# The second FFN's units set one unit further behind the first FFN's

## The chip, the cores and the metric

The kernel runs on one core of one Trainium2 chip. The metric is the device time of one execution in microseconds (us), lower is better; the median of several runs is given, and beside it one execution that the hardware profiler recorded.

## What is computed

For two batches of 3008 tokens of width 256, a squared-ReLU attention, then two feed-forward networks (FFNs) on all 6016 tokens:

```python
scores = (1.0 / S) * np.matmul(z, z.transpose(0, 2, 1))      # z: 64 wide
attn   = np.maximum(scores, 0.0) ** 2
x      = u * np.matmul(attn, v)                              # B*S = 6016 rows of 256
h      = x @ w_in                                            # 256 -> 2048
y      = (h - np.tanh(h)) @ w_out                            # 2048 -> 256
gate   = 1.0 / (1.0 + np.exp(-(y @ w_gate)))                 # 256 -> 1536
out    = (gate * (y @ w_val)) @ w2_out                       # 1536 -> 256
```

The FFN weights come as 64-bit floats and are decoded on the core. Each matmul of the FFNs is done as three matmuls of rounded high and low parts (names ending in h and l: yh, yl; gh, gl).

## The kernel before

The 6016 tokens are cut into 12 chunks (`chunks`): five of 512 tokens and one of 448 in each batch, so chunks 5 and 11 are short. All work on PE is cut into **units**, and the program is written unit by unit, in an order that a table of numbers sets.

- `Attention` and `HalfAttention`: two key tiles of a chunk, 12 units a chunk.
- `Ffn1(c, f)` (L391): 256 of the first FFN's 2048 inner columns of chunk c, 8 units a chunk. Its `front` (L399) is 12 matmuls into a PSUM tile `h`; `mid1` (L405) turns h into th (four instructions of ACT: th, sq, sq, m; three of DVE: e, th, th); `mid2` (L419) splits th into gh (ACT) and gl (DVE); `back` (L428) is 12 matmuls of gh and gl with w_out into two accumulators `acc` in PSUM. After the last unit of a chunk, `end` (L434) splits the accumulators into yh and yl, the input of the second FFN.
- `Ffn2(c, f)` (L443): 128 of the 1536 inner columns of chunk c, 12 units a chunk. `front` (L451) is 12 matmuls into `gv`; `mid1` one sigmoid on ACT (sg, L461) and one product on DVE (L462); `mid2` the split into p (ACT L467, DVE L81); `back` (L471) is 6 matmuls of p into its own pair of accumulators. After a chunk's last unit `end` (L474) copies the two accumulators to `o` with two ACT instructions (L479) and stores o with two DMAs of SP's queue (L480).

`accumulate` (L227, matmul at L235) and `project` (L243, matmul at L247) issue the FFNs' matmuls. The accumulators of both FFNs come from the pool `psa` (L72), which has two pairs of banks; a new pair is taken at the `back` of a chunk's first unit (L620 to L622). `front`'s tiles come from `psf`, also two.

The main loop takes one unit a step. In step n it writes, in this order: the helpers due at n (loads, splits of weights and of x), `front` and `mid1` of unit n, `mid2` of unit n-1, the `end` of a chunk whose last `back` was in the step before (`LATE` is 1), and `back` of unit n-3. Each engine runs its instructions in the order in which they are written.

The order of the units around the last attention chunk and in the FFNs is `mixed` (L486 to L490): every unit gets a number and the units are sorted by it, the first FFN ahead of the second at equal numbers. Unit f of chunk c of the second FFN has the number 19.5 + 12c + f + LAG; unit f of chunk c of the first FFN 19.5 + 12(c - 1) + 1.5f (for c of 1 and more). With LAG = 7 the last unit of a chunk of the second FFN (f = 11) and the first unit of its next chunk stand next to each other.

Loads of x (`load_x`, 8 units ahead of the first FFN's chunk) and its split (`split_x`, 3 units ahead) hang on the first FFN's units; the splits of the second FFN's weights (L561 to L564) on the second FFN's units of chunk 0, 3 units ahead. Weights, x, y and o live in 41 slots of the pool `ring`.

Of the kernel before, what the change touches and what calls it, by code (L numbers as in the profile page):

```python
# [30 lines left out]
def squared_relu_attention__then__two_ffns(  # L31
# [31 lines left out]
    SPLIT = 9  # L63
    START = 11.5
    LAST = 7.5
    LAG = 7

    ring = ctx.enter_context(tc.tile_pool(name="ring", bufs=41))
    work = ctx.enter_context(tc.tile_pool(name="work", bufs=10))
# [418 lines left out]
    mixed += [(KP + LAST + (c - 1) * N2 + f * N2 / N1, 1, Ffn1(c, f)) for c in range(1, NC) for f in range(N1)]  # L488
    mixed += [(KP + LAST + c * N2 + f + LAG, 2, Ffn2(c, f)) for c in range(NC) for f in range(N2)]
    units += [t[2] for t in sorted(mixed, key=lambda t: t[:2])]  # L490
# [178 lines left out]
```

## Time and profile before

| | |
|---|---|
| median of 3 runs | 1656.49 us (1656.0 to 1656.74) |
| the profiled execution | 1654.31 us, span 1652.5 us |
| PE busy | 1593.4 us, 96% of the span |
| DVE, ACT busy | 67%, 63% of the span |
| granted clock of PE, mean | 0.982 |
| DMA | 32 GB/s mean |

The span runs from the first to the last instruction. PE is the matrix engine, PEld its weight loads, DVE the vector, ACT the scalar engine; SP issues the DMAs. In a chain of waits, the work that ended last is followed back from the last instruction, at each step to what released it; a timeline lists the instructions in order of time and in brackets the idle time before them with what ended it. Granted clock 1.00 is 2.4 GHz, 0.50 is 1.2 GHz.

### The profile page before, as it was taken

How to read it: one execution, taken by the hardware profiler on the slowest of the kernel's cores; microseconds unless marked ns; L12 is line 12 of the kernel's file. 1: busy time of each engine (PE TensorE's matmuls, PEld its weight loads, DVE VectorE, ACT ScalarE, POOL GpSimd, SP SyncE). 2: the span in 40 equal slices, each digit the busy share in tenths (PEclk: the TensorE clock that was granted, in tenths of full speed). 3: DMA queues.
4: the chain of work that ended last, by engine and by line, in shares of the span. 5: the costliest groups of instructions: out<-in, count | busy, mean ns of one | idle time of the engine just before them, and what ended most of it. 6: DMA issues, size and time to landing. Idle time of an engine off the chain costs nothing.

```text
span 1652.5 us, 21852 instructions
## 1 busy us (share of the span) xinstructions
PE 1593.4 (96%) x9120; PEld 1371.7 (83%) x9120; DVE 1106.0 (67%) x1255; ACT 1038.4 (63%) x1251; POOL 0.2 (0%) x4
## 2 busy tenths in 40 slices
PE   9999999999999998998989989898998989989898
PEld 7888899999998887887878878787887878878788
DVE  8988889888789775564555555465555655656433
ACT  8767778776789776565555556566555656556422
POOL 0000000000000000000000000000000000000000
PEclk9999999999999999999999999999999999999999
DMA  6222232221010000000000000000000000000000
GB/s 217 78 78 77 83 109 76 77 78 52 25 39 25 0 1 13 26 1 24 1 13 13 1 26 0 24 3 12 13 1 26 0 13 12 0 13 0 13 1 24
DMA packets 28179, 53.31 MB, mean 32 GB/s; under 512 B 1968, under 2 KB 10160, under 8 KB 28080
## 3 DMA queue, kind: packets, MB, share of 16 engines
q1 hardware_dynamic: 28080, 51.91, 9.2%
q8 instruction: 71, 1.16, 0.3%
q14 instruction: 28, 0.23, 0.0%
HBM read 39.58 MB, written 12.32 MB: 31 GB/s over the span
## 4 chain that ended last, share of the span: by engine, by line
PE 93%; DVE 3%; ACT 3%; issue 1%; DVEq 0%; ACTq 0%
PE acc L235 27%; PE gv L247 24%; PE acc L364 22%; PE h L247 14%; PE s L321 6%; DVE th L416 1%; DVE th L417 1%; ACT sq L413 1%; DVE e L81 1%; DVE gl L81 1%; ACT sq L412 1%; ACT th L411 1%; ACT p L467 0%; ACT o L479 0%; PE acc L584 0%
## 5 line engine op out<-in xcount | busy, mean ns | idle before, releaser
L364 PE MATMUL acc<-ah,v 64*128 64x512 f32 (+1 forms) x2212 | 322.7, 383 | 0.0
L81 DVE TENSOR_TENSOR e<-h,th 128x1024 f32<-128x1024 f32 (+1 forms) x96 | 115.3, 1201 | 281.7 <-ACT sq L412 281.7
L235 PE MATMUL acc<-p,wo 128*128 128x512 f32 (+1 forms) x864 | 229.9, 404 | 52.5 <-ACT o L479 52.5
L364 PEld LDWEIGHTS acc<-ah,v 64*128 64x128 f32 x2212 | 246.7, 184 | 19.2
L235 PEld LDWEIGHTS acc<-p,wo 128*128 128x128 f32 x864 | 168.8, 197 | 89.1 <-ACT o L479 58.4
L461 ACT ACTIVATE sg<-gv 128x512 f32<-128x512 f32 (+1 forms) x144 | 84.6, 588 | 240.3 <-PE gv L247 240.1
L247 PE MATMUL h<-xh,wi 128*128 128x512 f32 (+1 forms) x768 | 233.7, 385 | 0.0
L411 ACT ACTIVATE th<-h 128x1024 f32<-128x1024 f32 (+1 forms) x96 | 96.8, 1008 | 210.9 <-PE h L247 210.9
L462 DVE TENSOR_TENSOR sg<-gv,sg 128x512 f32<-128x512 f32 (+1 forms) x144 | 97.7, 679 | 179.8 <-ACT sg L461 179.8
L235 PE MATMUL acc<-gh,wo 128*128 128x512 f32 (+1 forms) x768 | 204.2, 385 | 0.0
L364 PE MATMUL acc<-al,v 64*128 64x512 f32 (+1 forms) x1106 | 200.3, 383 | 0.0
L333 ACT ACTIVATE a<-s 128x1024 f32<-128x1024 f32 (+2 forms) x142 | 142.3, 1003 | 86.1 <-PE s L321 54.9
L81 DVE TENSOR_TENSOR al<-a,ah 128x1024 fp32r<-128x1024 f32 (+3 forms) x146 | 173.5, 1188 | 11.3 <-DVE ah L338 0.5
L247 PE MATMUL gv<-yh,wg 128*128 128x512 f32 (+1 forms) x576 | 180.1, 395 | 0.0
L247 PE MATMUL gv<-yh,wv 128*128 128x512 f32 (+1 forms) x576 | 175.7, 386 | 0.0
L247 PEld LDWEIGHTS h<-xh,wi 128*128 128x128 f32 x768 | 144.1, 188 | 27.5 <-ACT a L281 0.3
L235 PEld LDWEIGHTS acc<-gh,wo 128*128 128x128 f32 x768 | 144.2, 188 | 27.1
L336 ACT ACTIVATE a<-a 128x1024 f32<-128x1024 f32 (+2 forms) x142 | 147.7, 1041 | 4.4
L247 PE MATMUL h<-xl,wi 128*128 128x512 f32 (+1 forms) x384 | 147.9, 385 | 0.0
L364 PEld LDWEIGHTS acc<-al,v 64*128 64x128 f32 x1106 | 131.8, 184 | 9.8 <-DVE al L81 0.2
L417 DVE COPY_PREDICATED th<-m,e 128x1024 f32<-128x1024 uint32 (+1 forms) x96 | 131.2, 1366 | 9.9
L247 PEld LDWEIGHTS gv<-yh,wg 128*128 128x128 f32 x576 | 112.3, 195 | 21.8
(98 smaller groups left out, 2211.7 us busy)
## 6 DMA issues: line engine op xcount, KB each, us to landing
raw_wo<-w_out SPq DMA_DIRECT2D x14, 512.0 KB, 5.7
u<-uT SPq DMA_DIRECT2D x10, 512.0 KB, 6.7
x<-u SPq DMA_DIRECT2D x10, 512.0 KB, 3.0
xl<-x SPq DMA_DIRECT2D x10, 512.0 KB, 3.3
outT<-o SPq DMA_DIRECT2D x20, 256.0 KB, 2.1
vraw<-v SPq DMA_DIRECT2D x9, 512.0 KB, 6.9
raw_wi<-w_in SPq DMA_DIRECT2D x8, 512.0 KB, 8.2
zraw<-zT SPq DMA_DIRECT2D x12, 256.0 KB, 6.4
```

Source lines behind the costliest of these rows:

```text
L81: nc.vector.tensor_tensor(out=out, in0=a, in1=b, op=ALU.subtract)
L235: nc.tensor.matmul(acc[d][:, :n], wt[:, wi, w, d * P : (d + 1) * P], hl[ai], start=first and m == 0, stop=last and m == len(passes) - 1,)
L247: nc.tensor.matmul(ps, w[:, wi, d, fi * P : (fi + 1) * P], xs[xi][:, d, :n], start=m == 0, stop=m == len(passes) - 1)
L321: nc.tensor.matmul(self.ps[:, e, :n], z_t[b, i // 4][r, ki ^ x, c : c + P], q[r, qi ^ x, :n], start=m == 0, stop=m == 2)
L333: nc.scalar.activation(a[:, t, :n], self.ps[:, t, :n], AF.Relu, scale=SCALE)
L336: nc.scalar.activation(s, s, AF.Square)
L364: nc.tensor.matmul(acc[h][d][:, :n], vt[r, w, e, d * P : (d + 1) * P], self.hl[a][r, e, :n], start=self.first and banks[k] not in banks[:k ...
L411: nc.scalar.activation(t, h, AF.Tanh)
L412: nc.scalar.activation(s, h, AF.Tanh, scale=BETA)
L417: nc.vector.copy_predicated(t, m.bitcast(U32), e)
L461: nc.scalar.activation(s[:, :n], self.ps[:, 0, :n], AF.Sigmoid)
L462: nc.vector.tensor_tensor(out=s[:, :n], in0=self.ps[:, 1, :n], in1=s[:, :n], op=ALU.mult)
```

## The change

One constant is raised: every unit of the second FFN gets a number higher by one. Nothing is added or removed; the last unit of a chunk of the second FFN and the first of its next chunk now have one unit of the first FFN between them (for chunks 0 to 9; behind the first FFN's last unit only units of the second FFN are left).

```diff
@@ -63,7 +63,7 @@
     SPLIT = 9
     START = 11.5
     LAST = 7.5
-    LAG = 7
+    LAG = 8
```

What it does to the order is seen at three places.

First place: PE where chunk 0 of the second FFN ends and its chunk 1 begins. acc0_6760 and acc1_6761 before, acc0_6795 and acc1_6796 now, are chunk 0's accumulators; acc0_7436 before and acc0_7471 now are chunk 1's; h is the first FFN's `front`, gv the second's. Before:

```order
L235 MATMUL acc1_6761<-p_7330,wo2_5_7179 128x512 x3
L247 MATMUL h_7404<-xh2_6803,wi1_6_5945 128x512 x2
L247 MATMUL h_7404<-xl2_6619,wi1_6_5945 128x512
...
L235 MATMUL acc0_7436<-p_7363,wo2_0_6036 128x512
L235 MATMUL acc1_7437<-p_7363,wo2_0_6036 128x512
```

Now:

```order
L235 MATMUL acc1_6796<-p_7338,wo2_5_7219 128x512 x3
L247 MATMUL gv_7412<-yh1_6967,wg2_0_5948 128x512 x2
L247 MATMUL gv_7412<-yl1_6968,wg2_0_5948 128x512
...
L235 MATMUL acc0_7009<-gh_7369,wo1_5_5901 128x512
L235 MATMUL acc0_7009<-gl_7370,wo1_5_5901 128x512
...
L247 MATMUL gv_7452<-yh1_6967,wg2_1_6661 128x512 x2
L247 MATMUL gv_7452<-yl1_6968,wg2_1_6661 128x512
...
L235 MATMUL acc0_7471<-p_7403,wo2_0_6036 128x512
```

Before, one `front` of 12 matmuls stood between the last matmul into chunk 0's accumulators and the first into chunk 1's; now 36 stand there: a `front` of 12, a `back` of the first FFN of 12, and another `front` of 12.

Second place: ACT at the same boundary, around the two copies to o. Before:

```order
L411 ACTIVATE th_7418<-h_7404 128x1024
L412 ACTIVATE sq_7417<-h_7404 128x1024
L413 ACTIVATE sq_7417<-sq_7417 128x1024
L414 ACTIVATE m_7419<-sq_7417,square_max_71 128x1024
L467 CAST p_7428<-sg_7391 128x512
L479 COPY o0_7431<-acc0_6760 128x512
L479 COPY o0_7431<-acc1_6761 128x512
L461 ACTIVATE sg_7457<-gv_7444 128x512
```

Now:

```order
L411 ACTIVATE th_7393<-h_7379 128x1024
L412 ACTIVATE sq_7392<-h_7379 128x1024
L413 ACTIVATE sq_7392<-sq_7392 128x1024
L414 ACTIVATE m_7394<-sq_7392,square_max_71 128x1024
L467 CAST p_7403<-sg_7366 128x512
L461 ACTIVATE sg_7425<-gv_7412 128x512
L424 CAST gh_7428<-th_7393 128x1024
L479 COPY o0_7432<-acc0_6795 128x512
L479 COPY o0_7432<-acc1_6796 128x512
L221 CAST xh3_7449<-xl3_7287 128x1024
L461 ACTIVATE sg_7465<-gv_7452 128x512
```

The copies still stand behind the four instructions of a unit of the first FFN and a p, and now also behind a sigmoid and a gh; the split of x (xh3) comes behind them.

Third place: PE where the second FFN begins (chunk 0, unit 0), as a piece of the difference.

```order
-L247 MATMUL gv<-yh_6559,wg_0_5948 128x512 x2
-L247 MATMUL gv<-yl_6560,wg_0_5948 128x512
+L247 MATMUL h<-xh_6288,wi_5_5819 128x512 x2
+L247 MATMUL h<-xl_6083,wi_5_5819 128x512
 L235 MATMUL acc_6565<-gh,wo_2_5688 128x512
```

The `front` of the first FFN's chunk 1, unit 5 now stands where the first `front` of the second FFN stood, which comes one step later.

## Rows read from the trace of the kernel before

**Rows 1.** The page, busy time by engine over the whole span.

```profile
PE 1593.4 (96%) x9120; PEld 1371.7 (83%) x9120; DVE 1106.0 (67%) x1255; ACT 1038.4 (63%) x1251; POOL 0.2 (0%) x4
```

**Rows 2.** PE's waits: for whom, us in total, times, longest us.

```profile
PE acc L235 <- ACT o L479: 52.5, 10, 5.3
...
PE gv L247 <- DVE yl L81: 0.9, 1, 0.9
```

**Rows 3.** Chain of waits at the first boundary: start us, us, what.

```profile
653.50 2.73 PE h L247 x12
...
656.32 1.02 ACT th L411
...
660.43 0.60 ACT p L467
661.03 0.49 ACT o L479
...
661.57 2.99 PE acc L235 x6
664.56 3.05 PE gv L247 x12
```

**Rows 4.** Ten boundaries: stretch, its length, PE busy (instructions), granted clock, DMA share, GB/s.

```profile
656.23:667.61 11.38, 6.04 (x19) 0.70 0.12 46
756.02:768.59 12.57, 7.24 (x19) 0.73 0.11 42
...
1544.32:1555.16 10.84, 5.93 (x19) 0.84 0.13 49
sum 115.37, PE 62.97; mean PE 6.30
```

**Rows 5.** Two stretches: length, PE, PEld, DVE, ACT, POOL busy (instructions), granted clock, DMA.

```profile
8.00:473.00 465.00, 465.00 (x4165) 428.80 (x4166) 414.42 (x513) 349.66 (x401) 0.00 (x0) 1.00 0.25 84
545.00:655.00 110.00, 110.00 (x486) 91.07 (x487) 78.74 (x87) 76.43 (x95) 0.00 (x0) 1.00 0.02 6
```

**Rows 6.** Chain of waits inside a chunk, no boundary near.

```profile
707.05 2.72 PE h L247 x12
709.77 1.36 PE acc L235 x6
711.13 2.72 PE gv L247 x12
713.85 2.72 PE acc L235 x12
716.57 2.72 PE gv L247 x12
719.29 1.36 PE acc L235 x6
```

**Rows 7.** ACT's timeline: the copies to o, then the stretch of rows 6.

```profile
660.94 1.06 ACT L479 COPY o<-acc 128x512 f32<-128x512 f32 x2
...
714.50 0.59 ACT L461 ACTIVATE sg<-gv 128x512 f32<-128x512 f32 x1
715.93 1.06 ACT L424 CAST gh<-th 128x1024 fp32r<-128x1024 f32 x1 [0.85 <-DVE th L417]
719.32 0.60 ACT L461 ACTIVATE sg<-gv 128x512 f32<-128x512 f32 x1 [2.33 <-PE gv L247]
```

**Rows 8.** Chain of waits where the second FFN begins.

```profile
539.13 1.15 DVE e L81
...
544.20 0.61 DVE yl L81
...
544.86 2.56 PE gv L247 x10
```

**Rows 9.** PE behind the first FFN's last unit: length, busy, granted clock, DMA.

```profile
1579.50:1648.00 68.50, 68.50 (x326) 1.00 0.02 8
```

**Rows 10.** All engines' waits, the row of gh: us in total, times, longest us.

```profile
ACT gh L424 <- DVE th L417: 25.4, 35, 0.9
```

## The prediction

> **What bounds the kernel now.** I read the page's busy times first: PE is busy 1593.4 us of a span of 1652.5, DVE and ACT two thirds of it [rows 1]. PE sets the time, so the question is where the other 59 us lie. PE's waits answer it: 52.5 us, in ten waits of up to 5.3 us, are matmuls into acc at L235 that wait for the copies to o at L479 [rows 2]. These are the ten boundaries at which the second FFN goes from one chunk to the next while the first FFN still runs: chunk 1's first `back` wants the accumulators that chunk 0 leaves. With the first FFN holding one of the two pairs, the second has only one, and must wait until ACT has copied it out.
>
> The chain of waits tells why the copies are late [rows 3]. They are not long (1.06 us for both, [rows 7]); they are behind others. The `front` h ends at 653.50 + 2.73 = 656.23; then ACT does that unit's th, sq, sq and m from 656.32, a p at 660.43, and only then o. PE goes on at 661.57, 5.34 us after h ended. It does so slowly: its six matmuls take 2.99 us where six take 1.36 elsewhere, and the next twelve 3.05 where twelve take 2.72 [rows 3, 6]. The granted clock of these stretches is 0.70 to 0.84, against 1.00 in the long stretches where PE never rests [rows 4, 5]: part of each stop is at the lower of PE's two levels, and the first matmuls behind it too.
>
> **What the ten stops cost.** Each stretch of rows 4 runs from the end of the h before a stop to the end of the twelfth gv matmul behind it, and holds 18 matmuls. The ten are 10.84 to 12.57 us long, 115.37 in all. Without a stop 18 matmuls take 1.36 + 2.72 = 4.08 us [rows 6]. One of the ten stretches is of the short chunk 5, where 448 columns for 512 make it 4.08 x 448/512 = 3.57. Ten are thus worth 9 x 4.08 + 3.57 = 40.3, and the stops cost 115.4 - 40.3 = **75.1 us**: 52.5 of waiting [rows 2] and some 22 of slow matmuls and hand-over.
>
> The Trainium skill (TensorE: Matmul & The Clock Gate, HAM oscillation — how this bites in real kernels) prices the low clock otherwise: the throttled time times one half. With the mean granted clock of 0.982 that gives an estimate of 1652.5 x 0.018 / 0.5 = 59 us throttled, 30 us of penalty, and 52.5 + 30 = 82 us to win instead of 75, which would end at some 1573. I stay with the rows, since part of the throttled time is the waiting itself, which would be counted twice.
>
> **The change, part by part.**
>
> *The boundary.* Nothing is added or removed; 36 matmuls now lie between the last one into the old accumulators and the first into the new, not 12. Whether that hides the copies is read from a place in the trace where the units have the same kinds in the same order (second, first, second, first, second, second FFN) and no boundary is near. In rows 6 the `back` of 709.77 stands for the chunk's last and that of 719.29 for the next chunk's first. ACT's row there [rows 7]: gh, behind which the copies now stand, runs from 715.93 to 716.99, after having waited 0.85 for DVE; then ACT is idle until 719.32. The copies would take 716.99 to 718.05, and PE wants the bank at 719.29: 1.24 us to spare. The longest that gh ever waited for DVE is 0.9 [rows 10], so 0.85 is already near the worst. From above: if DVE were late by as much once more, the copies would end at 718.95, still in time. So I take a stop of zero, and the 75.1 us go, low clock included. Bounds: zero, and 1 us at each boundary for whatever these rows cannot show (10 us). The idle 2.33 us of ACT covers the copies, so what follows them on ACT is not late: the x split behind them (another cast, like gh some 1.06) would run to about 719.1, and the sigmoid of 719.32 stays.
>
> *The start of the second FFN.* PE now waits 0.9 us for yl, once [rows 2, 8]. A `front` of the first FFN (2.72 us) now stands there; its PSUM tile is free since the e of 539.13 ended at 540.28, so PE starts it at about 544.0, and yl is done at 544.8, long before it is needed. **0.9 us** goes. DVE has one more unit of the first FFN before the light ones begin: from e to yl one such unit takes 544.20 - 539.13 = 5.07 us of DVE [rows 8], against 5.44 us of PE for its `front` and `back` of 12 matmuls each [rows 6]; it keeps up. Should gl be late there, it costs about as much as is won: 0 to 0.9.
>
> *The end.* Behind the first FFN's last unit stand 21 units of the second, not 20. In that stretch PE is busy 68.50 of 68.50 us at clock 1.00 [rows 9], with the boundary to chunk 11 in it, which needs no copy in time since the first FFN's banks are free. One unit more is PE time that was spent elsewhere before: zero.
>
> *Moved with the units.* The splits of the second FFN's weights (units 2 and later) and the DMAs of o keep their distance to the units that use them, and SP's queue keeps its order. x is loaded 8 units ahead as before, now just before the `front` that frees the old y; 34 weights, two y, two x and this load are 34 + 4 + 2 + 1 = 41 slots, just the ring's 41, and if it had to wait for one `front` it would still be many units early. Zero. DVE and ACT, at 78.74 and 76.43 us of 110 in a chunk [rows 5], are no bound when PE runs through.
>
> **Sum.** 75.1 + 0.9 = 76.0 us. The profiled execution took 1654.31, so it would take 1578.3. It lies 2.2 us under the median of the runs, 1656.49; to that the sum is 1580.5, which I give.
>
> **Rivals.**
>
> *The copies are still a little late.* For it: they stand behind one more instruction that waits for DVE, and the margin is 1.24 us. Against: the same pattern has it in every chunk, and PE's stop is counted with it. Were PE to stop 1 us at each boundary, 10 us come back: 1590. So short a stop costs no clock: behind the 0.9 us at 544, clock and stretch are full [rows 5]. Chance 0.09.
>
> *A shorter stop, with the low clock.* If PE still stops 2.5 us at each boundary and the slow matmuls (22 us over ten, 2.2 each) come with it, 47 of the 75 us stay: 1656.49 - 28 - 1 = 1628. It takes copies that end 2.5 + 1.24 = 3.7 us later than in rows 7. Chance 0.03.
>
> *The wait does not move at all,* because chunk 1's accumulators are still wanted right behind the old ones. The order of the instructions speaks against it (36 matmuls). 1656, chance 0.02.
>
> *Slower: the copies fall behind DVE.* Before, they waited for ACT alone; now gh is ahead of them, which waits for DVE's last th. If PE, no longer resting at the boundaries, keeps DVE behind, every us of that delays the copies. It decides from where the stop exceeds the old 5.3: DVE late by 5.3 + 1.24 = 6.5 us, more than one unit of the first FFN (5.07). With two units (10.1) the stop is 8.9, with 2.2 for the slow matmuls 11.1 against 7.5 now: 10 x 3.6 = 36 us slower, 1692. For it: DVE was behind at 544 [rows 8]. Against: 79 of 110 us busy, and gh never waits over 0.9 [rows 5, 10]. Chance 0.02.
>
> **How the numbers follow.** My forecast has 0.84, with a range of its own of 1577 to 1585: the sum against the profiled execution and against the median, and a few tenths a boundary. For 8 in 10 I go from 1576 to 1590, which takes in most of the first rival. A measurement of this kernel tells about 0.2% (3.3 us) from no change. Faster by more: the forecast and the first two rivals, 0.96; within it 0.02; slower 0.02.
>
> **What would show it.** In the profile after, PE has no wait for o at L479, or one of tenths of a us; busy time down by the slow matmuls' excess, 62.97 - 40.3 = 22.7 us [rows 4], to about 1571, over 99% of a span of 1576.5; granted clock 1.00 at every boundary and 0.99 or more in the mean; no wait for yl; gh's waits for DVE still under 1 us. A row of ten waits for o, of a us or more, or a clock under 1.00 at the boundaries, would show the margin on ACT misread. A new wait of PE for gl or p, spread over the chunks, would say that DVE or ACT cannot follow an unresting PE, and the forecast would be wrong there.

## The result and the profile after

The changed kernel takes **1577.71 us** (median of 5 runs, 1577.35 to 1578.33) against 1656.41 (5 runs beside it): a ratio of 0.9527, with a 95% interval of 0.9513 to 0.9541. The forecast was 1580.5 with a range of 1576 to 1590. The profiled execution took 1577.74 us, its span is 1576.0, which is 76.5 us less than before; the sum of the prediction was 76.0.

The page of the changed kernel, busy time by engine, answers to [rows 1]; below it the chain that ended last, by engine:

```profile
PE 1570.5 (100%) x9120; PEld 1353.7 (86%) x9120; DVE 1105.8 (70%) x1255; ACT 1038.3 (66%) x1251; POOL 0.2 (0%) x4
...
PE 100%; DVE 0%; issue 0%
```

The work is the same (9120 matmuls), but PE's busy time fell by 22.9 us, and of the 59 us in which it stood still 5.5 are left. The waits of [rows 2] are gone; the only one that is listed now stands at the very start of the program, where it stood before as well:

```profile
PE acc L584 <- DVE blank L573: 1.5, 1, 1.5
```

The chain of waits through the same boundary as in [rows 3], with chunk 0's last `back` at 650.96 and chunk 1's first at 660.48, does not leave PE:

```profile
648.24 2.72 PE h L247 x12
650.96 1.36 PE acc L235 x6
652.32 2.72 PE gv L247 x12
655.03 2.72 PE acc L235 x12
657.75 2.72 PE gv L247 x12
660.48 1.36 PE acc L235 x6
```

ACT's timeline of these microseconds shows what the prediction read from [rows 6, 7], now with the copies in their place:

```profile
655.69 0.59 ACT L461 ACTIVATE sg<-gv 128x512 f32<-128x512 f32 x1
657.11 1.05 ACT L424 CAST gh<-th 128x1024 fp32r<-128x1024 f32 x1 [0.84 <-DVE th L417]
658.07 1.07 ACT L479 COPY o<-acc 128x512 f32<-128x512 f32 x2
659.02 1.06 ACT L221 CAST xh<-xl 128x1024 fp32r<-128x1024 f32 x1
660.51 0.60 ACT L461 ACTIVATE sg<-gv 128x512 f32<-128x512 f32 x1 [0.43 <-PE gv L247]
```

The copies end at 658.07 + 1.07 = 659.14; PE wants the accumulators at 660.48: 1.34 us to spare. The cast of x behind them still ends before the next sigmoid. The granted clock of everything from the first FFN on (windows view: stretch, length, PE busy, clock, DMA) is 1.00, where the boundaries had 0.70 to 0.84 [rows 4]:

```profile
474.00:1571.00 1097.00, 1097.00 (x4927) 1.00 0.03 11
```

### The profile page after: what moved, and what is told of

Its sections match the earlier page's. It is cut to its first block, busy times and chain, and to the rows that moved or that the text cites. A ratio compares the mean times of both kernels' runs of the same rounds, so it can differ in the third digit from the quotient of the medians.

```text
span 1576.0 us, 21857 instructions
## 1 busy us (share of the span) xinstructions
PE 1570.5 (100%) x9120; PEld 1353.7 (86%) x9120; DVE 1105.8 (70%) x1255; ACT 1038.3 (66%) x1251; POOL 0.2 (0%) x4
## 4 chain that ended last, share of the span: by engine, by line
PE 100%; DVE 0%; issue 0%
PE acc L235 29%; PE gv L247 24%; PE acc L364 24%; PE h L247 16%; PE s L321 6%; PE acc L584 0%; DVE o L479 0%; DVE blank L573 0%; DVE square_max L571 0%
## 5 line engine op out<-in xcount | busy, mean ns | idle before, releaser
L364 PE MATMUL acc<-ah,v 64*128 64x512 f32 (+1 forms) x2212 | 316.3, 383 | 0.0
L364 PEld LDWEIGHTS acc<-ah,v 64*128 64x128 f32 x2212 | 236.8, 184 | 22.3
L235 PE MATMUL acc<-p,wo 128*128 128x512 f32 (+1 forms) x864 | 215.5, 386 | 0.0
L364 PE MATMUL acc<-al,v 64*128 64x512 f32 (+1 forms) x1106 | 192.9, 383 | 0.0
L235 PEld LDWEIGHTS acc<-p,wo 128*128 128x128 f32 x864 | 162.3, 188 | 29.9
L247 PE MATMUL gv<-yh,wg 128*128 128x512 f32 (+1 forms) x576 | 175.3, 386 | 0.0
L364 PEld LDWEIGHTS acc<-al,v 64*128 64x128 f32 x1106 | 123.9, 184 | 11.1 <-DVE al L81 0.2
L247 PEld LDWEIGHTS gv<-yh,wg 128*128 128x128 f32 x576 | 108.2, 188 | 20.1
```

The lines of the kernel that those rows point to most:

```text
L235: nc.tensor.matmul(acc[d][:, :n], wt[:, wi, w, d * P : (d + 1) * P], hl[ai], start=first and m == 0, stop=last and m == len(passes) - 1,)
L247: nc.tensor.matmul(ps, w[:, wi, d, fi * P : (fi + 1) * P], xs[xi][:, d, :n], start=m == 0, stop=m == len(passes) - 1)
L364: nc.tensor.matmul(acc[h][d][:, :n], vt[r, w, e, d * P : (d + 1) * P], self.hl[a][r, e, :n], start=self.first and banks[k] not in banks[:k ...
```

## Experiments

My theory: the copies to o were late because of what stood before them on ACT; parting the chunks gives PE enough other work meanwhile; and a stop costs more than its waiting. Its rivals: the greater distance of the two FFNs is what helps, or 12 matmuls are too few whatever ACT does, or all of the cost is waiting.

### Distance kept, parting undone: adjacent8

```diff
-    mixed += [(KP + LAST + c * N2 + f + LAG, 2, Ffn2(c, f)) for c in range(NC) for f in range(N2)]
+    mixed += [
+        (KP + LAST + c * N2 + f + LAG - (0.6 if f == 0 and 0 < c < NC - 1 else 0), 2, Ffn2(c, f))
+        for c in range(NC)
+        for f in range(N2)
+    ]
```

> The change kept (every unit of the second FFN one later) but the first unit of chunks 1 to 10 put right behind the old chunk's last unit again, so that nothing parts them. Theory (the parting is what helps): the copies to o end some 4 to 5 us after PE wants the accumulators, ten stops and the slow matmuls behind them come back, 1640 to 1660 us. Rival (the greater distance of the second FFN from the first is what helps): 1576 to 1582 us.

Measured: 1640.45 us (0.9908 of before, 0.9893 to 0.9923). The ten waits are back. PE's waits, and the chain at the first boundary:

```profile
PE acc L235 <- ACT o L479: 40.5, 10, 4.4
```

```profile
655.99 1.35 DVE th L417
...
657.36 1.04 ACT gh L424
658.41 0.49 ACT o L479
...
658.94 2.99 PE acc L235 x6
661.93 4.10 PE gv L247 x12
```

One number in the table undoes 63 of the 79 us with all else of the change in place; the distance alone gives little. The edit does one thing more: it puts two units of the first FFN in a row behind the boundary. That is the prediction's slower rival at work in small: gh waits for DVE's th, and the copies wait behind gh.

### Nearer, but parted: lag6

```diff
-    LAG = 7
+    LAG = 6
```

> LAG 6: the second FFN is nearer than before, and its chunks are parted, by unit 4 of the first FFN, with the copies still behind four ACT instructions of the next first-FFN unit. Theory: h ends, PE has 24 matmuls (5.44 us) before it wants the accumulators, the copies end 5.3 us after h: no stop or one of a tenth of a us, 1577 to 1581 us, the wait of 0.9 us for yl there as with LAG 7. Rival (distance helps): slower than with LAG 7, over 1656 us.

Measured: 1583.3 us (0.9562, 0.9548 to 0.9576), 2.3 us over the range expected, but 72 under before. So moving the second FFN *nearer* also wins, as long as a unit parts its chunks. What is left over shows in the weight loads' timeline at the first boundary:

```profile
656.15 0.19 PEld L235 LDWEIGHTS acc<-p,wo 128*128 128x128 f32 x1 [0.34 <-ACT o L479]
656.63 0.99 PEld L235 LDWEIGHTS acc<-p,wo 128*128 128x128 f32 x5 [0.30 <-ACT o L479]
```

I had reckoned with one end of the copies. There are two: the first matmul goes into the first accumulator, the second into the other, whose copy ends 0.5 us later. lag6_sorted, below, tests that.

### Chunks adjacent, copies earlier on ACT: early7

The `end` of the second FFN's chunk goes ahead of the step's `mid1`; LAG stays 7.

```diff
+            if pending and n >= pending[0][0] and isinstance(pending[0][1], Ffn2):
+                _, u, a = pending.pop(0)
+                u.end(a)
             if n < total and near and isinstance(units[n], HalfAttention):
                 units[n].mid1(later=True)
```

> LAG 7, chunks adjacent, but the copies to o are written ahead of the four ACT instructions of the step's own unit. Theory (the copies were late only because of what stood before them on ACT): ACT is idle for some 2.4 us before that unit's th, the copies fit there, no stop, 1577 to 1580 us. Rival (12 matmuls are too few for the accumulators to be emptied, wherever the copies stand): a stop of 2 us or more at each boundary, over 1600 us.

Measured: 1578.66 us (0.9534, 0.9518 to 0.955). Neither distance nor parting was needed: with the same 12 matmuls between the chunks the copies run in ACT's idle time ahead of th, and PE does not stop. ACT's timeline (the `front` before th ends at 655.72 in the chain):

```profile
652.37 1.06 ACT L424 CAST gh<-th 128x1024 fp32r<-128x1024 f32 x1
653.33 1.06 ACT L479 COPY o<-acc 128x512 f32<-128x512 f32 x2
655.82 1.03 ACT L411 ACTIVATE th<-h 128x1024 f32<-128x1024 f32 x1 [1.43 <-PE h L247]
```

What it has over the changed kernel is the wait for yl, still 0.9 us at the start of the second FFN; its median is 0.95 us longer and its span 0.8.

### What a stop costs, waiting and clock apart: filler7

LAG 7 with the stops, but PE is given 20 useless matmuls in each (the next unit's PSUM tile is taken early and written over by its `front`; the lines that hand the tile on are left out here).

```diff
+                if isinstance(u, Ffn2) and u.first and 0 < u.c < NC - 1:
+                    ps = psf.tile([P, 2, NQ], F32, tag="f", name="gv")
+                    units[n + 1].given = ps
+                    wt = w_t["wo1_", 0]
+                    for _ in range(20):
+                        nc.tensor.matmul(
+                            ps[:, 0], wt[:, 0, 0, :P], wt[:, 0].rearrange("p t f -> p (t f)"), start=True, stop=True
+                        )
                 u.back(acc)
```

> LAG 7 with the stops kept, but PE does 20 matmuls without use (4.5 us) into the next unit's PSUM tile during each of the ten. It separates the waiting from the clock. Theory (75 us are 53 of waiting and 22 of slow matmuls): the clock stays at 1.00 at the boundaries, the slow matmuls' 22 us go, the waiting stays: 1632 to 1637 us. Rival (all of it is waiting): 1656 us. By the estimate of 30 us from the mean clock: 1626 us.

Measured: 1636.94 us (0.9885, 0.9871 to 0.99). Adding 200 matmuls that compute nothing makes the kernel 18.7 us faster. PE's waits, and three stretches of the windows view (before the first stop, the filled stop, behind it):

```profile
PE acc L237 <- ACT o L481: 7.3, 10, 0.8
```

```profile
545.00:655.00 110.00, 110.00 (x487) 1.00 0.02 6
655.50:660.90 5.40, 4.57 (x21) 1.00 0.00 0
660.86:668.21 7.35, 7.35 (x31) 1.00 0.19 71
```

The fillers take 200 x 2.72/12 = 45.3 us, which with the 7.3 of waiting left is the old waiting (52.6 against 52.5). The clock holds at 1.00 through the stop and behind it. So the 75 us split into 52.5 of waiting, 18.7 of low clock, and some 4 to 5 of something else: filler7's span, 1634.7, less the changed kernel's 1576.0, 45.3, 7.3 and yl's 0.9 leaves 5.2, half a us a boundary.

The trace of the kernel before agrees. Here are its first stop and the 18 matmuls behind it (windows view):

```profile
656.23:661.57 5.34, 0.00 (x1) 0.69 0.00 0
661.57:667.61 6.04, 6.04 (x19) 0.71 0.23 87
```

Over the ten boundaries the stops have a clock of 0.69 to 0.99, and the stretches of matmuls behind them 0.58 to 0.74. With time at the lower level counted as length x (1 - clock) / 0.5, an estimate from these windows, the low clock lasts 58 us in all: 16 while PE waits, 42 while it works. Only the 42 cost time, half of them, 21 us; 18.7 were measured.

### Eating up the margin: late2, late4, late10

The changed kernel, with 2, 4 or 10 more copies ahead of the two that count:

```diff
             o = slot([ND, NQ], F32, f"o{self.c}")
+            for _ in range(4 if self.c < NC - 2 else 0):
+                nc.scalar.copy(o[:, 0, :n], acc[0][:, :n])
```

> The changed kernel with two more ACT copies (1.06 us) ahead of the two to o at each of the ten boundaries. Theory (the copies end 1.3 us before PE wants the accumulators): 0.3 us to spare, no stop, 1577 to 1579 us. If the margin is smaller than read, up to 10 us more.

> The same with four more copies (2.1 us). Theory: PE stops about 0.8 us at each of ten boundaries, too short for a lower clock: 1585 to 1588 us. Rival (even a short stop brings slow matmuls): 1600 us or more. Rival (margin larger than read): 1578 us.

> The same with ten more copies (5.3 us). Theory: stops of about 4 us at ten boundaries, and the lower clock with them (some 2 us each): 1630 to 1640 us. Rival (linear, no clock): 1617 us.

Measured: 1579.02 (0.9539, 0.9526 to 0.9552), 1590.22 (0.9606, 0.9593 to 0.9619) and 1645.72 us (0.9943, 0.9931 to 0.9956). late2 lies at the upper end of what I expected: two more copies bring no listed wait and cost next to nothing, so a margin of over 1.1 us is there. late4 lies 2 us and late10 6 us over what I expected. For late10, part of the miss is the size of a copy: the timeline's 1.06 us for two overlaps them, while in a row they come 0.62 us apart, as late10's chain shows at its first boundary:

```profile
658.56 0.49 ACT o L478
...
659.08 0.60 ACT o L478
659.69 0.60 ACT o L478
...
664.63 0.59 ACT o L481
...
665.27 2.99 PE acc L235 x6
668.26 3.44 PE h L247 x12
```

Ten are thus 6.1 us, not 5.3. For late4 the size is not the cause: its copies are longer too (2.5 us, not 2.1), but its waits add up to 6.8 us, less than the 8 expected. What was too small there is the price of a stop. PE's waits, of late4 and then of late10:

```profile
PE acc L235 <- ACT o L481: 6.8, 10, 1.2
```

```profile
PE acc L235 <- ACT o L481: 43.5, 10, 5.0
```

late4's 6.8 us of waiting cost 12.5 us of time. Its clock is not the cause: the mean of its whole execution is 1.000. At its first boundary PE goes on at 661.40, and the stretch behind that has 1.00 (windows view). In late10 PE goes on at 665.27, and its first six matmuls run at 0.50:

```profile
661.40:666.03 4.63, 4.63 (x19) 1.00 0.30 113
```

```profile
665.27:668.26 2.99, 2.99 (x7) 0.50 0.47 175
```

### The second copy: late4_sorted and lag6_sorted

The first unit of a chunk of the second FFN puts its three matmuls into one accumulator and then three into the other, instead of in turn:

```diff
-            if last:
+            if last or first and self.kind == 2:
                 order.sort(key=lambda o: o[1])
```

> The kernel with four more copies, and the first unit of each chunk of the second FFN fills its accumulators one after the other (three matmuls into the first, then three into the second) instead of in turn. Theory (part of what a stop costs beside the wait is the second copy, which ends 0.5 us after the first and holds up PE's second matmul): the first three matmuls cover most of it, 3 to 5 us less than without, 1585 to 1588 us. Rival (the first matmuls behind a stop are slow for another reason): 1590 us as without.

> LAG 6 with the same order of the first unit's matmuls. Theory: of the 4.5 us lost at its boundaries to two weight loads that wait 0.3 us each, one for each copy, the second's part goes, 1580 to 1582 us. Rival: 1583 us as without.

Measured: 1587.54 us (0.9587, 0.9574 to 0.96) against 1590.22 without, and 1580.66 (0.9545, 0.9532 to 0.9558) against 1583.3. Both save 2.6 to 2.7 us, late4_sorted a little less than the 3 expected. In late4_sorted PE still waits 6.8 us in all, but the six matmuls behind the first stop take 1.67 us instead of 1.92:

```profile
661.57 1.67 PE acc L235 x6
```

In lag6_sorted the first boundary's weight loads wait once instead of twice:

```profile
656.22 1.23 PEld L235 LDWEIGHTS acc<-p,wo 128*128 128x128 f32 x6 [0.34 <-ACT o L479]
```

So about half of what those two kernels lose beside the listed waits is the second copy. The other half is not explained by an experiment. It is 0.31 us at the first stop of late4_sorted (1.67 against 1.36), and [rows 8] had as much in the kernel before: ten gv matmuls behind the wait for yl took 2.56 us, where ten of twelve in 2.72 take 2.27. The weight loads suggest a reason. In the changed kernel they start at 660.09, 0.2 us ahead of the first matmul; in late4_sorted, the second line, the first of them waits for the copy too and starts with its matmul, at 661.57:

```profile
660.09 1.32 PEld L235 LDWEIGHTS acc<-p,wo 128*128 128x128 f32 x6
661.57 1.24 PEld L235 LDWEIGHTS acc<-p,wo 128*128 128x128 f32 x6 [1.13 <-ACT o L481]
```

None of the runs is faster than the changed kernel.

## Why the prediction was right

- **What bounds the kernel.** Ten waits for o were nearly all that PE lost, and they are gone; the time fell by their price. early7 shows the reading of [rows 3] by itself: the copies were late for what stood ahead of them on ACT.
- **The price of a stop.** 75.1 us was right to about a us: 76.5 less span, of which the second FFN's start has 0.9. The step that set slow matmuls and hand-over beside the waiting at 22 us stands, and filler7 splits it: 18.7 for the clock, the rest mostly hand-over. The estimate of 30 us of penalty, worked out from the mean clock by the Trainium skill (TensorE: Matmul & The Clock Gate, HAM oscillation — how this bites in real kernels), was too high by 11 us here. As the prediction said, part of the throttled time was PE waiting: some 16 of 58 us by the windows above, which takes 8 us off the 30; the last 2 to 3 stay open. Its words that part of each stop is at the lower level are too broad: two of the ten stops had a clock of 0.99.
- **The margin.** The copies were put at 1.24 us before PE's need, from a stretch without a boundary; they came 1.34 before it, and late2 (no stop) and late4 (stops of up to 1.2) close it in from both sides. The reading was on the safe side: PE's first matmul needs only the first copy, and late4's 2.5 us of copies for 0.7 us of waiting put the margin to that one at some 1.8 us (an estimate). gh's waits for DVE, said to stay under 1 us, now reach 1.0, and there are 44 of them instead of 35; they cost PE nothing.
- **The start of the second FFN.** The 0.9 us for yl went; early7 and lag6 keep it.
- **The end and what moved with the units.** Nothing there shows: PE is busy for 1097.00 of 1097.00 us from 474 on.
- **The rivals.** The first priced a stop of 1 us at 1 us; by late4, 0.7 us a boundary costs 1.25. That term was too small, by the second copy and by about as much again that [rows 8] already showed, though it did not come to bear. The slower rival's point of decision was copies 6.5 us late; late10, with 6.1, is 0.6% faster than before, which agrees.
- **The time.** 1577.71 lies 2.8 us under the forecast. 2.2 of that is the offset that I carried from the profiled execution of before to its median; the profiled execution after lies on its median. By medians the gain is 78.7 us, between the 76.0 of the rows and the 83 (82 and 0.9) of the estimate from the mean clock; the time alone would not have told which price was right, filler7 does. All runs of the kernel before spread over 1652.95 to 1658.44, those of the changed kernel over 1 us. That the length of the slow stretch at each stop, 10.84 to 12.57 us in one execution [rows 4], differs from run to run would explain it, but was not tested.

## What to carry to other kernels

When a matrix engine waits for a short copy out of PSUM, look at what stands before the copy in its engine's queue: here 1 us of work cost 7.5 us because five instructions of other units were ahead of it. Either put other matmuls between the last use of an accumulator and its next, or write the copy ahead of work that must wait anyway; both gave the same time to within 1 us. Judge a new place for a copy by an undisturbed stretch with the same order of kinds of work, with its margin, and price a stop by the whole stretch until the matmuls are back at full pace, not by the listed wait.

## What the runs showed of the hardware that I had not expected

A wait that the trace lists as 0.7 us on average cost 1.25 us with the clock at 1.00. With two accumulators filled in turn, the second matmul waits for the second copy, and the listed wait of the first does not hold that; ordering the matmuls took away about half of the excess. The other half, some 0.3 us a stop, was not tested.

Expected in size (1632 to 1637 us), but worth knowing: two hundred useless matmuls in the stops made the kernel 18.7 us faster (1636.94 against 1655.68). The clock then stayed at 1.00, and the six matmuls behind the first stop, which itself was as long as before, took 1.91 us instead of 2.99:

```profile
660.86 1.91 PE acc L237 x6
```
